# RWKV time mixing and a Fourier-mixed MLP on one core: the transposes of the last two batches made by DMA instead of TensorE

## The chip, the core and the metric

The kernel runs on one core of a Trainium2 chip. A core has five engines with a queue of instructions each: PE (TensorE, matrix products out of SBUF into PSUM), ACT (ScalarE), DVE (VectorE), POOL (GpSimd) and SP (SyncE, which here only issues DMAs). An engine takes its instructions strictly in order; between engines there are only semaphores. Transfers run on 16 DMA engines that all queues share. PSUM has 8 banks of 128 x 512 fp32, and only PE, ACT and DVE reach it in this kernel. The metric is device time in microseconds (us) of one execution; lower is better.

## The reference, cut to what matters

```python
# attention, (batch, heads, seq, head_dim) = (4, 8, 768, 48), one state matrix per head
for t in range(S):
    cur = einsum('bhd,bhe->bhde', u * kt, vt)
    y[:, :, t] = einsum('bhd,bhde->bhe', rt, state + cur)
    state = wt[..., None] * state + einsum('bhd,bhe->bhde', kt, vt)
# y is laid out as x (4, 768, 384), then
X = fft(fft(x, axis=1), axis=2)
u = x + real(X)
un = (u - mean(u)) / sqrt(var(u) + 1e-6)       # over the 384 features
out = u + relu(un @ w_ch1) @ w_ch2             # w_ch1 384 x 1536, w_ch2 1536 x 384
```

## The kernel before

**Attention.** Each batch has six chunks of 128 time steps, 24 chunks in all; chunk number n is 6 times the batch plus the chunk in the batch. A chunk's r, k, v and w arrive as four loads of 192 KB (L546), each in rows of 48 floats (192 bytes). The logarithm of w (L516, tile `lb`) is summed over time by two triangular matmuls (L707, L711) and exponentiated (L713, L726); r and k are multiplied by the results into bf16 tiles `rh` (L745, DVE) and `kh` (L502, mostly POOL), 128 time steps x 512 columns (8 heads padded to 64). TensorE contracts over partitions, so the product of k with r needs both with the head dimension on partitions: four transposes each of 128 x 128 against the identity (L756 for r, L762 for k) go to a PSUM bank, and one copy each (L525 on ACT or L526 on DVE) takes the bank to the SBUF tiles `rtb` and `ktb`. Eight matmuls (L773) then give the 128 x 128 products, DVE masks them into `ah` (L778), and the state (L796, L799, L807) and the output (L820, L823, L829) follow. L820 also reads `rtb`.

**Mix and MLP.** When a batch's six chunks are done, the Fourier transforms are matmuls against tables (L884 to L910). Each of six blocks of 128 rows is added to x (L912), its mean and variance are taken (L916, L918), the centred rows go to a bf16 tile `un` of 128 x 384 (L516 on ACT or L507 on DVE), three transposes on PE (L929) and one copy (L525 or L526) put them into `unt`. Three blocks make a half batch: 36 matmuls of the first layer (L951), the negative ReLU (L958 ACT, L956 DVE) and 36 of the second (L969), then the sum with u (L973) and the store (L977).

**Order.** Every instruction is recorded as an operation with its tiles. The order on each engine's queue is not found at run time: it is written out in the table `ORDER`, one list of operation numbers for each engine. At build time `schedule` walks those lists with assumed durations, only to assign PSUM banks, and `emit` puts a semaphore wait in front of an operation for what it depends on. So the engines run fixed lists, and a late operation holds everything behind it on its engine. SP's list holds all loads and stores; the weights of the two MLP layers are two DMAs on POOL's list (L685).

**Buffers.** There are 7 buffers for each loaded tensor and 3 each of `rh`, `kh`, `rtb` and `ktb`.

**The opening.** PE starts with 18 matmuls on scratch data (L990), and 20 pairs of matmuls whose result nobody reads (L1017, 384 columns each) are spread over its list in about the first 45 us.

Of the kernel before, what the change touches and what calls it, by code (L numbers as in the profile page):

```python
# [21 lines left out]

W_AFTER = {"W1": (0, 3, "w"), "W2": (1, 0, "r")}

W0, WP, NW = 8.0, 1.6, 20
# [4 lines left out]
        "72 6 99 125 127 1474 124 101 151 98 1475 153 64 68 137 111 110 136 114 203 1476 140 117 1477 177 179 "  # L30
        "143 150 119 205 163 176 66 189 162 145 1478 169 166 1479 188 1480 261 1481 1482 192 1483 202 171 215 "
        "195 228 229 262 197 214 1484 454 218 239 425 240 427 1485 456 243 1486 223 263 221 424 483 1487 1488 "
        "264 253 453 246 254 485 255 265 256 257 269 270 271 272 273 258 274 443 275 276 277 278 279 266 280 "
        "1489 437 292 301 436 302 303 283 293 294 284 465 312 285 313 466 330 314 1490 472 331 469 1491 332 1492 "
        "1493 440 308 299 321 290 322 323 475 361 341 347 349 482 355 345 357 351 353 337 343 328 359 446 363 "
        "495 319 365 370 366 494 512 511 371 498 501 514 367 386 382 372 523 504 380 384 545 524 546 548 530 390 "
        "527 557 388 375 558 533 578 564 376 579 561 775 377 777 398 589 394 590 392 396 566 593 402 400 404 774 "
        "596 804 787 603 604 405 611 619 806 786 803 406 790 620 605 606 621 622 623 612 607 608 624 625 626 627 "
        "613 614 628 629 630 615 616 651 793 815 633 642 652 653 634 635 643 644 662 409 816 833 663 832 835 410 "
        "411 822 819 414 664 658 415 640 649 796 416 825 695 693 709 713 697 845 844 851 699 701 691 848 711 896 "  # L40
        "862 864 898 705 669 703 671 672 861 673 895 707 854 715 874 929 716 873 680 717 681 877 725 907 880 908 "
        "720 940 682 911 883 721 928 1154 914 726 1156 1125 1127 678 916 722 939 1124 687 727 943 742 730 740 "
        "750 732 736 752 1183 738 734 953 1137 954 1143 946 1136 1185 744 746 1153 748 764 765 1140 1166 969 "
        "1165 1172 955 766 956 961 970 1169 957 971 972 973 1182 958 974 962 975 976 963 977 964 965 978 979 980 "
        "1201 1146 966 1212 992 1214 1195 1001 983 984 985 993 1002 1211 994 1003 1194 1012 759 1175 1246 754 "
        "1013 1014 1224 760 761 1198 1021 1022 1008 755 1279 999 1248 1230 990 1023 756 1245 1223 1204 1063 1053 "
        "1047 1041 1227 1043 1045 1030 1055 1031 1032 1257 1057 1233 1278 1051 1049 1258 1061 1070 1264 1028 "
        "1261 1059 1075 1289 1071 1290 1266 1065 1019 1293 1076 1066 1311 1037 1303 1067 1312 1077 1296 1082 "
        "1072 1090 1304 1319 1086 1096 1313 1094 1102 1305 1314 1320 1084 1321 1306 1322 1307 1315 1323 1316 "
        "1324 1308 1325 1092 1100 1342 1326 1327 1351 1328 1329 1333 1330 1088 1080 1098 1362 1334 1335 1371 "  # L50
        "1352 1104 1380 1343 1344 1353 1114 1363 1115 1364 1109 1381 1382 1372 1340 1110 1105 1373 1106 1358 "
        "1349 1111 1116 1401 1407 1403 1413 1411 1387 1395 1393 1369 1405 1397 1378 1391 1399 1432 1436 1444 "
        "1452 1440 1450 1430 1409 1415 1448 1420 1442 1434 1425 1446 1416 1421 1426 1422 1438 1427 1417 1459 "
        "1460 1461 1454 1464 1455 1456 1465 1466 1469 1470 1471"),
    "act": (
        "0 73 20 21 22 23 24 25 26 97 123 149 128 126 102 154 100 60 65 59 138 201 107 133 175 69 180 152 178 "
        "165 206 159 164 191 185 423 67 227 204 452 217 231 230 216 236 481 241 242 211 433 428 455 486 250 426 "
        "259 457 267 260 462 268 282 438 445 467 468 439 298 307 289 309 300 362 342 348 310 350 346 358 327 354 "
        "356 344 352 484 339 497 474 510 496 491 513 515 520 311 503 387 544 525 381 547 549 385 554 532 559 577 "
        "560 580 340 773 581 389 391 591 592 778 395 539 397 393 399 586 802 776 401 789 403 841 788 783 602 572 "  # L60
        "805 807 609 631 617 831 817 812 632 795 818 836 834 657 639 860 648 659 660 650 641 894 904 696 824 710 "
        "870 698 847 846 700 714 692 712 927 702 899 865 661 704 670 863 708 1123 897 931 876 853 909 910 942 "
        "882 1152 677 936 930 1181 679 686 941 1157 1126 1128 1210 889 689 731 1133 922 743 733 741 1162 737 739 "
        "735 1139 1191 1186 1138 1145 690 1155 747 749 751 952 1168 1167 1174 1220 959 1184 981 967 960 1244 "
        "1197 1215 1196 1213 1277 1203 1286 1226 998 1007 989 1009 1000 991 1010 1247 1281 1018 1249 1011 1048 "
        "1064 1042 1044 1046 1056 1259 1254 1232 1280 1052 1027 1050 1060 1239 1291 1062 1020 1036 1272 1038 "
        "1029 1083 1087 1091 1302 1309 1103 1093 1097 1331 1101 1317 1081 1039 1339 1357 1040 1360 1350 1341 "
        "1386 1370 1408 1379 1406 1404 1445 1414 1392 1361 1389 1398 1443 1437 1451 1390"),
    "dve": (
        "32 52 7 30 41 62 33 27 31 8 39 5 28 38 29 44 10 15 36 9 42 43 11 12 13 14 35 61 17 16 48 34 18 19 54 45 "  # L70
        "56 63 37 103 53 129 57 104 55 58 105 134 135 109 108 131 155 112 113 139 116 115 142 118 141 157 144 "
        "120 160 183 186 146 213 167 190 170 168 194 193 212 172 196 198 237 209 219 220 234 245 224 222 244 226 "
        "199 247 463 434 249 458 459 444 281 460 429 304 295 305 286 287 296 288 297 306 315 333 471 470 291 324 "
        "316 442 334 325 326 317 476 335 336 431 441 318 338 360 432 364 473 492 320 447 329 488 489 500 521 502 "
        "499 368 518 383 505 526 555 531 529 528 373 552 534 587 536 565 562 588 535 563 378 584 595 594 567 538 "
        "569 597 784 599 598 570 600 571 601 813 792 794 791 654 636 645 637 655 638 656 646 407 412 647 821 665 "
        "820 842 666 781 823 667 810 668 797 694 839 826 852 867 849 850 868 706 840 869 674 902 855 871 417 875 "
        "675 905 676 879 878 718 881 683 913 884 684 912 937 685 915 886 917 688 723 1131 919 945 934 887 1134 "
        "1160 728 944 753 1144 947 745 949 948 1163 1141 1142 1173 1171 1170 767 1147 1202 1192 986 995 1004 987 "
        "996 1005 997 1221 1006 988 1176 1015 762 1200 1199 1016 1189 1024 757 1017 1231 1255 1225 1218 1288 "  # L80
        "1205 1229 1228 1025 1054 1284 1026 1234 1252 1058 1260 1287 1265 1263 1033 1262 1237 1292 1034 1267 "
        "1035 1268 1294 1295 1285 1068 1270 1297 1298 1073 1271 1299 1078 1300 1085 1095 1099 1336 1089 1332 "
        "1354 1337 1345 1338 1355 1346 1356 1365 1366 1347 1383 1348 1384 1359 1374 1385 1375 1376 1367 1117 "
        "1368 1112 1402 1107 1412 1377 1388 1396 1394 1400 1431 1410 1453 1433 1441 1447 1449 1435 1439 1423 "
        "1428 1418 1462 1457 1467 1472"),
    "pool": (
        "4 1 2 3 51 46 50 130 40 47 161 156 49 181 132 182 106 187 158 122 184 121 207 208 148 147 232 174 238 "
        "233 210 173 200 235 225 251 435 248 464 252 430 493 461 487 490 516 517 522 519 550 556 551 553 582 583 "
        "537 585 785 568 610 808 814 809 837 618 779 838 780 843 782 811 866 932 900 901 872 903 1129 906 938 "
        "1130 1158 1159 933 885 918 1135 935 1164 888 1132 921 920 951 950 1193 1187 1161 982 968 1222 1188 1216 "  # L90
        "1250 1282 1217 1190 1219 1283 1251 1256 1236 1235 1253 1238 1269 1301 1310 1318"),
    "sp": (
        "71 77 75 78 74 79 70 81 82 87 83 80 89 86 76 85 84 90 88 92 419 91 448 93 94 477 96 420 95 422 449 478 "
        "450 421 451 479 506 480 507 508 509 540 542 541 543 573 769 575 574 770 576 771 828 798 772 830 827 801 "
        "800 374 799 829 369 856 893 923 924 859 891 890 858 379 857 925 892 1120 1121 1119 1149 1273 1180 408 "
# [286 lines left out]
def bass_rwkv6_finch__then__fnet_fourier_mix_kernel(  # L382
# [93 lines left out]
    def ps(t):  # L476
        return BANK[t.bank]
# [575 lines left out]
```

## Time and profile before

| what | value |
|---|---|
| median of 3 runs | 194.43 us (193.92 to 194.43) |
| the profiled execution | 194.31 us, of which the span of its profile is 192.5 us |
| PE | busy 181.3 us, 94% of the span, 1802 matmuls |
| DVE | 165.1 us, 86% |
| ACT | 131.7 us, 68% |
| POOL | 104.8 us, 54% |
| HBM | 23.59 MB read, 4.72 MB written |

Busy means that an instruction of the engine runs. PE's matmuls are pipelined: one of 128 columns is listed with 219 ns, but the next can start some 55 ns after it, so for PE the distance between starts is what a matmul costs. The span runs from the first to the last instruction of the profile; 1.8 us of the execution lie outside it.

### The profile page before, as it was taken

The numbers are of one execution on the slowest core, as the hardware profiler recorded it, in microseconds if no ns is written. First come the engines' busy times: TensorE is split into PE (matmuls) and PEld (weight loads), VectorE is DVE, ScalarE is ACT, GpSimd is POOL, SyncE is SP. The second block draws the span as 40 slices with busy tenths as digits, with TensorE's granted clock in tenths as the row PEclk, the third lists the DMA queues.
The fourth block names the chain that finished last, engine by engine and source line by source line (L and its number), as shares of the span: only waits on it lengthen the run. The fifth ranks groups of instructions, "written<-read, shape, count | busy, mean of one in ns | idle before, by whom it ended". The sixth has DMA issues, their size and how long they took to land.

```text
span 192.5 us, 4725 instructions
## 1 busy us (share of the span) xinstructions
PE 181.3 (94%) x1802; PEld 119.6 (62%) x1802; DVE 165.1 (86%) x374; ACT 131.7 (68%) x307; POOL 104.8 (54%) x123
## 2 busy tenths in 40 slices
PE   5886998899999988999999999999999999999994
PEld 2353766576666655667667676866666766665663
DVE  7888899999998999999999988999989939955353
ACT  4895877397887968998977898997944273243200
POOL 4069889673009856499799597976952230000000
PEclk9997899999999999999999999999999999999999
DMA  5999998999979999899949985102000300120033
GB/s 115 211 214 199 191 222 156 202 202 206 200 143 210 220 183 243 176 236 191 225 102 215 245 182 134 44 0 69 18 0 3 123 0 5 41 82 3 0 130 115
DMA packets 105416, 26.26 MB, mean 136 GB/s; under 512 B 100273, under 2 KB 105010, under 8 KB 105394
## 3 DMA queue, kind: packets, MB, share of 16 engines
q1 hardware_dynamic: 103442, 23.60, 57.4%
q0 software_dynamic: 1952, 2.36, 7.3%
q8 instruction: 14, 0.23, 0.5%
q14 instruction: 8, 0.07, 0.1%
HBM read 23.59 MB, written 4.72 MB: 147 GB/s over the span
## 4 chain that ended last, share of the span: by engine, by line
PE 78%; DVE 10%; SPq 6%; DMA 2%; issue 2%; ACT 1%; DVEq 0%
PE bank L969 24%; PE bank L951 24%; SPq L546 5%; PE bank L910 5%; PE bank L887 3%; PE bank L773 3%; DMA in_v<-in_v_dram 2%; PE bank L762 2%; DVE ah L778 2%; PE bank L823 2%; PE bank L929 2%; PE bank L756 2%; PE bank L707 2%; PE bank L799 2%; PE bank L820 2%; PE bank L711 2%
## 5 line engine op out<-in xcount | busy, mean ns | idle before, releaser
L969 PE MATMUL bank<-w,ht 128*128 128x384 bf16 (+2 forms) x300 | 55.1, 319 | 0.0
L951 PE MATMUL bank<-unt,w 128*128 128x384 bf16 x288 | 54.1, 326 | 0.0
L958 ACT ACTIVATE ht<-bank 128x384 bf16<-128x384 f32 x69 | 31.6, 496 | 11.2 <-PE bank L951 10.9
L969 PEld LDWEIGHTS bank<-w,ht 128*128 128x128 bf16 x300 | 27.5, 98 | 15.0 <-DVE ht L956 0.2
L951 PEld LDWEIGHTS bank<-unt,w 128*128 128x128 bf16 x288 | 26.4, 98 | 15.1
L778 DVE TENSOR_TENSOR ah<-bank,msk 128x512 bf16<-128x512 f32 x48 | 31.5, 680 | 1.6 <-PE bank L773 1.3
L502 POOL TENSOR_TENSOR vtd<-in_v,dc 128x384 f32<-128x384 f32 x20 | 17.2, 858 | 14.8 <-DVE dc L734 14.5
L502 POOL TENSOR_TENSOR rk<-rk,ub 128x384 f32<-128x384 f32 x20 | 20.5, 1032 | 7.8 <-DVE rk L502 7.4
L956 DVE TENSOR_SCALAR ht<-bank 128x384 bf16<-128x384 f32 x27 | 14.2, 549 | 12.2 <-PE bank L951 12.2
L502 POOL TENSOR_TENSOR kh<-in_k,e 128x384 bf16<-128x384 f32 x19 | 20.0, 1053 | 5.5 <-ACT e L726 5.4
L502 POOL TENSOR_TENSOR rk<-in_r,in_k 128x384 f32<-128x384 f32 x19 | 19.5, 1030 | 2.8 <-DVE dc L734 2.7
L973 DVE SCALAR_TENSOR_TENSOR osb<-bank,rstd,uf 128x384 f32<-128x384 f32 (+2 forms) x25 | 14.7, 593 | 4.1 <-PE bank L969 4.1
L525 ACT ACTIVATE rtb<-bank 128x512 bf16<-128x512 bf16 x20 | 12.0, 599 | 4.7 <-PE bank L756 4.5
L713 ACT ACTIVATE bank<-bank 128x384 f32<-128x384 f32 x24 | 11.8, 493 | 4.6 <-PE bank L707 4.4
L829 DVE TENSOR_TENSOR x<-bank,vtd 128x384 f32<-128x384 f32 x24 | 13.1, 547 | 1.2 <-PE bank L823 0.9
L745 DVE TENSOR_TENSOR rh<-bank,in_r 128x384 bf16<-128x384 f32 x24 | 13.1, 546 | 1.0 <-ACT bank L713 1.0
L516 ACT ACTIVATE vb<-in_v 128x384 bf16<-128x384 f32 x24 | 12.5, 525 | 2.1 <-DMA in_v<-in_v_dram 2.1
L912 DVE TENSOR_TENSOR uf<-bank,x 128x384 f32<-128x384 f32 x24 | 12.8, 547 | 0.6 <-PE bank L910 0.4
L525 ACT ACTIVATE unt<-bank 128x384 bf16<-128x384 bf16 x17 | 7.9, 491 | 7.8 <-PE bank L929 7.4
L734 DVE TENSOR_REDUCE dc<-rk 128x8 f32<-128x384 f32 x24 | 13.0, 540 | 0.2 <-POOL rk L502 0.2
L516 ACT ACTIVATE un<-uf,agg 128x384 bf16<-128x384 f32 x18 | 10.5, 608 | 3.8 <-DVE agg L918 3.8
L916 DVE BATCH_NORM_STATS2 bst<-uf 128x6 f32<-128x384 f32 x24 | 12.6, 546 | 0.1
(134 smaller groups left out, 383.2 us busy)
## 6 DMA issues: line engine op xcount, KB each, us to landing
in_w<-in_w_dram SPq DMA_DIRECT2D x24, 192.0 KB, 3.9
in_r<-in_r_dram SPq DMA_DIRECT2D x24, 192.0 KB, 3.8
in_k<-in_k_dram SPq DMA_DIRECT2D x24, 192.0 KB, 3.7
in_v<-in_v_dram SPq DMA_DIRECT2D x24, 192.0 KB, 3.8
out_dram<-osb SPq DMA_DIRECT2D x23, 192.0 KB, 2.0
w<-in_moe_w_ch_dram POOLq DMA_DIRECT2D x2, 1152.0 KB, 11.7
out_dram<-osb SPq DMA_DIRECT2D x1, 128.0 KB, 1.7
out_dram<-osb SPq DMA_DIRECT2D x1, 64.0 KB, 1.6
```

Source lines behind the costliest of these rows:

```text
L502: return lambda e: e.tensor_tensor(out=o, in0=a, in1=b, op=f)
L516: return lambda e: e.activation(o, a, f, **kw)
L525: {"act": lambda e: e.activation(o(), i(), ACTF.Copy), "dve": lambda e: e.tensor_copy(out=o(), in_=i())}, **kw)
L734: op("dve", v_1(DM), lambda e: e.tensor_reduce(out=dc[:, :], in_=rku[:, :, :], axis=mybir.AxisListType.X, op=ALU.add), r=[("RK", i2)], w=[ ...
L745: op("dve", v_1(DM), lambda e: e.tensor_tensor(out=rh[:, :, 0:D], in0=ps(tce)[:, 0:DM].rearrange("t (h d) -> t h d", d=D), in1=rt[:, :, :] ...
L778: masked[n] = op("dve", v_1(512), lambda e, x=x: e.tensor_tensor(out=ah[:, x:H:2, :], in0=ps(ta[x])[:, :].rearrange("p (h t) -> p h t", t= ...
L829: op("dve", v_1(DM), lambda e: e.tensor_tensor(out=xb[:, c, 0:DM], in0=ps(ty)[:, 0:DM], in1=vtd[:, :, :].rearrange("t h d -> t (h d)"), op ...
L951: ins = e.matmul(ps(t)[:, 0:384], W1[:, m, 128 * j:128 * j + 128], unt[:, m, :], start=(m == 0), stop=(m == NM - 1))
L956: {"dve": lambda e, j=j, t=t, ht=ht: e.tensor_scalar(out=ht[:, j, :], in0=ps(t)[:, 0:384], scalar1=-1.0, scalar2=0.0, op0=ALU.mult, op1=AL ...
L958: "act": lambda e, j=j, t=t, ht=ht: e.activation(ht[:, j, :], ps(t)[:, 0:384], ACTF.Relu, scale=-1.0)},
L969: ins = e.matmul(ps(t)[:, 0:hi - lo], ht[:, j, 128 * x:128 * x + 128], W2[:, j, lo:hi], start=(j == 0), stop=(j == NJ - 1))
L973: op("dve", v_1(hi - lo) + 64, lambda e, kb=kb, t=t, o=o, lo=lo, hi=hi: e.scalar_tensor_tensor(out=o[:, lo:hi], in0=ps(t)[:, 0:hi - lo], s ...
```

## The change

In chunks 12 to 23 (batches 2 and 3; `DMA_T = 12`) the eight PE transposes of `rh` and `kh`, their two PSUM banks and their two copies are gone. In their place SP issues two DMAs that transpose from SBUF to SBUF: `rh` to `rtb`, `kh` to `ktb`, each 128 x 512 in blocks of 128 columns. For batches 2 and 3 (`DMA_U = 2`) the three transposes of each `un` and the copy are replaced by one such DMA of 128 x 384. The new DMAs stand in SP's list, between loads and stores. `rh`, `kh`, `rtb` and `ktb` get a fourth buffer.

The matmuls that nobody reads become 14 single ones instead of 20 pairs, placed in other positions. The copy of the broadcast u (`UB`) must now come after the load of the second activation table. All five lists of `ORDER` are new, so operations that are otherwise untouched stand in other places, the opening included.

```diff
+DMA_T, DMA_U, T_ISSUE, T_XFER = 12, 2, 900, 600
-W0, WP, NW = 8.0, 1.6, 20
+NW = 14
 ORDER = {
...
+    NT = 4 if DMA_T < B * NC else 3
-    RH = [sb("rh%d" % i, [H, 64], BF16) for i in range(NB)]
+    RH = [sb("rh%d" % i, [H, 64], BF16) for i in range(NT)]
...
-        o = evict(lambda: UB[:, :, :]..., r=[t], w=["UB"])
+        o = evict(lambda: UB[:, :, :]..., r=[t, "LOGEXP"], w=["UB"])
...
+        if n >= DMA_T:
+            for x, o, i, y in ((rT, "RTB", rflat, "RH"), (kT, "KTB", kflat, "KH")):
+                op("sp", T_ISSUE, lambda e, x=x, i=i: e.dma_start_transpose(out=x[:, :, :], in_=i), r=[(y, i4)], w=[(o, i4)],
+                   sem="%s%d" % (o, i4), xfer=T_XFER)
+        else:
+            trr, trk = g.tile("a"), g.tile("a")
...
+            if b >= DMA_U:
+                op("sp", T_ISSUE, lambda e, un=un, unt=unt, kb=kb: e.dma_start_transpose(
+                    out=unt[:, :, 128 * (kb % 3):128 * (kb % 3) + 128], in_=un[:, :]),
+                   r=[("UN", n % 3)], w=[("UNT", (2 * b + hf) % 2, kb % 3)], sem="UNT%d" % (n % 6), xfer=T_XFER)
+            else:
+                tu = g.tile("f")
...
     for i in range(NW):
         def warm(e):
-            for x in range(2):
-                ins = e.matmul(ps(tw)[:, 0:384], MSK[:, :], IDW[:, :])
-            return ins
-        o = op("pe", mm(384, 2), warm, r=["MSK", "IDB"], w=[tw])
-        o.ready0 = int(1e3 * (W0 + WP * i))
+            return e.matmul(ps(tw)[:, 0:384], MSK[:, :], IDW[:, :])
+        o = op("pe", mm(384), warm, r=["MSK", "IDB"], w=[tw])
```

`T_ISSUE` and `T_XFER` are durations that `schedule` assumes for a transposing DMA; they set no instruction's time.

## The prediction

> **What bounds the kernel now.** I read the engines' shares and the slices first, then the windows, the chain of waits, PE's list in time, and the DMA queue.
>
> ```profile
> PE 181.3 (94%) x1802; PEld 119.6 (62%) x1802; DVE 165.1 (86%) x374; ACT 131.7 (68%) x307; POOL 104.8 (54%) x123
> DMA  5999998999979999899949985102000300120033
> PE 78%; DVE 10%; SPq 6%; DMA 2%; issue 2%; ACT 1%; DVEq 0%
> ```
>
> ```profile
> 0.00:60.00 60.00, 52.65 (x543) 33.53 (x544) 54.33 (x142) 44.18 (x97) 34.00 (x51) 0.97 1.01 189
> 60.00:120.00 60.00, 58.72 (x659) 39.69 (x659) 57.61 (x116) 52.23 (x127) 47.74 (x50) 1.00 0.94 198
> 120.00:192.50 72.50, 69.94 (x606) 46.34 (x606) 53.11 (x118) 35.27 (x85) 23.01 (x24) 1.00 0.12 42
> ```
>
> The windows' columns are PE, PE's weight loads, DVE, ACT and POOL busy, PE's granted clock, the DMA share and GB/s. From 60 us on PE has no room left, so a matmul removed there is time saved. In the same 60 to 120 us the DMA engines are full too (0.94); only after 120 us are they free (0.12). The change moves work from the full PE to a resource that is full for half of the affected time. In the first 60 us PE idles 7.4 us and is held by loads.
>
> **PE's transposes.** Starts in PE's list, in the full stage:
>
> ```profile
> 118.13 0.40 PE L762 MATMUL bank<-idw,kh 128*128 128x128 bf16 x4
> 118.37 0.25 PE L887 MATMUL bank<-cs,xf 128*128 128x193 bf16 x1
> 118.45 0.39 PE L756 MATMUL bank<-idw,rh 128*128 128x128 bf16 x4
> 118.67 0.33 PE L799 MATMUL bank<-vb,kh 128*128 128x96 bf16 x4
> ...
> 164.21 0.50 PE L929 MATMUL bank<-idw,un 128*128 128x128 bf16 x6
> 164.54 1.46 PE L969 MATMUL bank<-w,ht 128*128 128x384 bf16 x8
> ```
>
> Four transposes hold PE for 118.67 - 118.45 = 0.22 us, six of L929 for 0.33, so three for 0.165. Removed: 12 chunks x 2 x 0.22 = 5.3 us and 12 x 0.165 = 2.0 us, together 7.3 us, all behind 70 us, where PE is full. Bounds: a saving of 7.3, and none if PE then waits as long for the DMAs. I take -7.3 and cost the waits below.
>
> **Copies.** 24 copies of `rtb` and `ktb` at about 0.60 us (ACT) and 12 of `unt` at 0.49 leave ACT and DVE, some 20 us. I cost this at nothing: PE's matmuls cover it. If the cover went, DVE (57.61 of 60) would be next, and the copies off it are some slack there.
>
> **The DMA's own time.** No row shows a transposing DMA. The nearest is the load stage, by the DMA view of 60 to 118 us:
>
> ```profile
> DMA packets 53990, 11.84 MB, mean 204 GB/s; under 512 B 52830, under 2 KB 53982, under 8 KB 53982
> q1 hardware_dynamic: 53982, 11.73, 96.0%
> ```
>
> 58 us x 0.96 x 16 engines / 53982 = 16.5 ns a packet. A load (1024 rows of 192 bytes) is 64 packets an engine, 1.06 us. If a transpose moves one packet for each 128 bf16 columns of a row (256 bytes), 128 x 512 is 32 packets an engine, 0.53 us, and 128 x 384 is 0.40. The other end: if it is cut into 32-byte pieces, it has eight times the packets, 4.2 us. I take 0.55, because a 256-byte row is the packet nearest to the 192-byte rows that were measured, and keep both ends.
>
> What fits: without transposes the loads end at 118.8 (last issue 114.99, landing 3.8 later); the last L773 of attention starts at 144.6 and must come to about 138 if the gain is to be had. So 30 transposes (24, and 6 of batch 2's rows) share about 19 us of DMA time: 0.63 us each. Below that the DMA costs nothing, since the free stretch after 120 us takes it up; above it every 0.1 us costs 3 us. At 0.55 it fits by 2.5 us.
>
> **SP's queue and the added waits.** SP issues 36 more DMAs. An issue takes 0.33 us when the queue is empty (stores after 150 us) and 0.7 to 1.0 when it is full; bounds 0.33 to 1.5, taken 0.9; SP is idle after 120 us. But each transposing DMA waits on SP's list for its `rh` or `kh`, and the loads and stores behind it wait with it: the first transpose is SP's 62nd DMA, and 36 loads of batches 2 and 3 stand behind it, between the others. L773, with all of PE's list behind it, waits for the landing. Before, one such path is
>
> ```profile
> 117.51 0.54 DVE L745 TENSOR_TENSOR rh<-bank,in_r 128x384 bf16<-128x384 f32 x1
> 119.06 0.59 ACT L525 ACTIVATE rtb<-bank 128x512 bf16<-128x512 bf16 x1
> 119.92 0.40 PE L773 MATMUL bank<-rtb,ktb 48*128 48x128 bf16 x8
> out_dram<-osb SPq DMA_DIRECT2D x9, 192.0 KB, 3.2
> ```
>
> 1.9 us from `rh` to L773. The fourth line is the store's landing in the same full queue, 3.2 us. So a chunk's path grows by 1.3 us. Bounds: 0 (L745 stands far enough ahead) and 12 x 1.3 = 15.6 us (nowhere). PE's list holds MLP matmuls between, of 0.16 us each in hundreds, and `rh` has a fourth buffer to run ahead, so I stay near the low end: +1.5.
>
> **The opening.** On POOL's new list the first weights' DMA stands behind an `rk` product that waits for `in_r` buffer 6, and that load is now SP's 36th issue. Rows of before:
>
> ```profile
> 33.58 0.87 SPq L546 DMA_DIRECT2D in_r<-in_r_dram  x1
> 34.01 0.97 POOL L685 DMA_DIRECT2D w<-in_moe_w_ch_dram  x1
> 47.30 0.97 PE L951 MATMUL bank<-unt,w 128*128 128x384 bf16 x5
> ```
>
> The 36th issue starts at 33.58 and lands some 3.8 later, and the product takes 1.0: the weights would be asked for near 38 us instead of 34.01, and land 10.5 to 12.9 later, near 50 against the 47.30 at which L951 now starts. That is some 4 us, partly filled by attention matmuls. The ends are -1 (the new order of the loads helps chunk 0, whose `v` was waited for until 16.79) and +5. I take +3.0. The broadcast of u goes from SP's first issue to its ninth and stands ahead of the first L707, which was at 10.4; it lands near 10.4 too, which lies in the same delay. The 26 dropped filler matmuls (0.16 us each, 4.2 us) stood in idle time: nothing, but for the clock:
>
> ```profile
> 14.00:16.00 2.00, 1.01 (x15) 1.00 1.14 222
> 16.00:18.00 2.00, 0.95 (x14) 0.80 0.99 189
> 18.00:20.00 2.00, 2.00 (x21) 0.50 0.98 196
> 20.00:25.00 5.00, 5.00 (x68) 0.94 1.00 195
> ```
>
> These windows are of PE alone: busy, clock, DMA share, GB/s. After a half-idle stretch the granted clock is 0.80 and then 0.50, and it comes back by 25 us. Fewer fillers and a PE that waits for u may bring a second such stretch; 2 us at half clock lose 1 us of matmuls, but the opening is held by loads, so I take nothing for it, with 0 and +1 as ends. The Trainium skill, "TensorE: Matmul & The Clock Gate", Part 1, says that an idle window of about 3.4 us halves the clock, which speaks against dropping fillers; by that rule the sum below would be 192.5 us. The trace agrees in kind, with the 0.50 above.
>
> **Sum**, against the profiled 194.31 us (0.12 below the median): -7.3 (PE) +3.0 (opening) +1.5 (late landings) + 0 (DMA, copies, fillers) = -2.8, so 191.5 us.
>
> **Rivals.**
> (1) The DMA engines become the bound, slower. It decides when one transpose costs the 16 engines more than 0.63 us, and the whole is slower from about 0.63 + 2.8/30 = 0.72 us on. For it: 0.94 in the load stage, and a load's 16 parts that do not finish together, so that a transpose which needs all engines at once would hold those that are early. Against: 16.5 ns a packet. At 0.9 us each the cost is 30 x 0.27 = 8 us: 199.6 us; at 1.3 us, 211.6. The Trainium skill, "VectorE: DVE Perf Modes", "The three transpose paths", gives 1309 ns for one 128 x 128 block by DMA and 390 ns on TensorE and so advises TensorE; it stands on this rival's side.
> (2) The transposes are hidden but late: SP's waits hold loads back and L773 comes late in most chunks. For it: 3.2 us of landing against a 1.9 us path, and no slack in PE's list. Against: after 120 us a store lands in under 2 us. Half of the 15.6 us bound is +7.8 instead of +1.5: 197.8; at +4.5 it is 194.5, no change. I place it at 195.
> (3) The pieces are 32 bytes: 24 x 4.2 + 12 x 3.2 = 139 us more DMA work, with 19 us of room; over 300 us.
>
> **How the numbers follow.** 0.3% (0.6 us) is about what a measurement can tell here. My forecast, 189 to 193.8: 0.49. Rival 1, 196 to 212: 0.32. Rival 2, 193 to 198: 0.16. Rival 3: 0.03. Faster: nearly all of the forecast and a little of rival 2, 0.50; the same: 0.07; slower: 0.43. Range: the low end 188.8 (opening at +0.3 instead of +3.0), which leaves out 0.05; the high end 204 takes in rival 2 and the lower half of rival 1, up to about 1.05 us each, and leaves out 0.14. The likeliest case's own range is 189 to 193.8.
>
> **What the profile after would show.** Right: PE busy near 170 us, no rows for L929 in batches 2 and 3, PE still full from 60 us to the end, the transposing DMAs landing in 3 us or less, loads ending near 135 us, first L951 near 50 us. Rival 1: DMA share at 9 in all slices to 140 us and beyond, and idle PE ended by DMA `rtb` or `ktb`. Rival 2: the same waits, but gaps in the DMA row. Wrong altogether: if the issue itself holds SP for several us, which no row of before can show.

## The result and the profile after

The changed kernel is slower: 201.76 us median against 194.18 us of the kernel before on the same chip, a ratio of 1.039 (95% interval 1.036 to 1.042), where 191.5 us was forecast. Its profiled execution took 201.77 us, with a span of 200.0 us. Some executions, of the kernel before too, take over 1.5% longer than the fastest of the same kernel; the times below are medians of the others.

From the page of the changed kernel, the engines' shares, the slices of the granted clock and of the DMA engines, and the chain of waits:

```profile
PE 179.1 (90%) x1644; PEld 112.4 (56%) x1644; DVE 157.9 (79%) x353; ACT 120.0 (60%) x285; POOL 109.6 (55%) x132
PEclk9955999999999999999999889999699999999999
DMA  6999999999999975989998996987754011415033
...
PE 52%; DMA 16%; DVE 11%; ACT 6%; SPq 6%; POOL 5%; issue 3%; DVEq 0%; POOLq 0%; ACTq 0%
```

DVE and ACT did get rid of 7 and 12 us. PE's share of the chain fell from 78% to 52%, and transfers hold 16% of it, against 2% before. The windows of the changed kernel behind 60 us (PE, weight loads, DVE, ACT and POOL busy, granted clock, DMA share, GB/s):

```profile
60.00:120.00 60.00, 54.82 (x553) 34.99 (x552) 51.76 (x105) 41.42 (x102) 41.41 (x43) 0.97 0.91 183
120.00:200.00 80.00, 73.57 (x589) 46.19 (x586) 53.54 (x116) 35.59 (x89) 26.46 (x28) 0.98 0.44 101
```

Behind 60 us PE was idle for 3.8 us before (132.5 - 58.7 - 69.9); now it is idle for 11.6 us (140 - 54.8 - 73.6). The largest waits, in the list of waits of PE behind 60 us, and the transposing DMAs in the DMA view (median us from issue to landing at the end of the line):

```profile
PE bank L779 <- DMA rtb<-rh: 3.8, 3, 1.9
PE bank L962 <- DMA unt<-un: 2.2, 1, 2.2
```

```profile
rtb<-rh SPq DMA_TRANSPOSE x12, 2.5
...
unt<-un SPq DMA_TRANSPOSE x12, 2.4
```

Six of the 11.6 us are waits for transposing DMAs. Behind the two longest of them the granted clock falls as well (windows of PE alone: busy, clock, DMA share, GB/s):

```profile
113.00:117.00 4.00, 4.00 (x16) 0.58 1.03 242
140.00:144.00 4.00, 4.00 (x16) 0.57 0.75 163
```

The first stretch stands right behind a wait of 1.9 us for `rtb`, which ends at 112.4 us, and the second behind the 2.2 us for `unt`, which end at 139.4 us. A mean of 0.58 over 4 us is half clock for 3.4 us, so 1.7 us of matmul work are lost in each. In the kernel before, the clock is 1.00 from 25 us on.

The landings are as short as hoped. What is late is the issue. SP's queue in the timeline of the changed kernel (start, duration, instruction):

```profile
139.15 1.21 SPq L756 DMA_TRANSPOSE rtb<-rh  x1
140.40 0.58 SPq L548 DMA_DIRECT2D in_k<-in_k_dram  x1
141.02 1.56 SPq L756 DMA_TRANSPOSE ktb<-kh  x1
142.62 0.58 SPq L988 DMA_DIRECT2D out_dram<-osb  x1
143.25 1.22 SPq L756 DMA_TRANSPOSE ktb<-kh  x1
144.51 0.58 SPq L548 DMA_DIRECT2D in_r<-in_r_dram  x1
```

Each row begins 0.04 or 0.05 us after the end of the one ahead: SP waits for nothing here, it is busy issuing. A transposing DMA holds it for 1.2 to 1.3 us (1.56 in one row here, right behind a load), and a plain DMA behind one for 0.58. From 75 to 153 us this goes on almost without a gap, while in the kernel before SP's rows in 118 to 153 us are six stores. They are merged into one row, which holds the idle time between them too; each takes 0.33 to 1.01 us of issue:

```profile
122.20 29.95 SPq L977 DMA_DIRECT2D out_dram<-osb  x6
```

What the full queue does to chunk 22 is seen in three rows of the changed kernel, and in one of the kernel before, which stands last:

```profile
141.33 0.52 DVE L747 TENSOR_TENSOR rh<-bank,in_r 128x384 bf16<-128x384 f32 x1
149.03 1.27 SPq L756 DMA_TRANSPOSE rtb<-rh  x1
151.66 0.40 PE L779 MATMUL bank<-rtb,ktb 48*128 48x128 bf16 x8 [0.95 <-DMA rtb<-rh]
...
140.72 0.40 PE L773 MATMUL bank<-rtb,ktb 48*128 48x128 bf16 x8
```

`rh` is ready at 141.85, its transposition is issued 7.2 us later, and the eight matmuls of the chunk's products (L773 before, L779 now) start at 151.66 instead of 140.7. Loads stand in the same queue and come late too: POOL, which had no such waits behind 60 us before, waits 4.6 us there for `in_k` and 4.6 us for `in_r`.

The lag grows in two steps. The first half batch of the MLP's first layer (L951 before, L962 now) ends 3.6 us later than before, the next two 2.3 and 2.6, the fourth to the sixth 6.0, 6.7 and 8.5, and the last 9.2. So the opening costs about 3 us, as forecast, and another 6 us are lost between 97 and 157 us, just where 7 us should have been gained.

### The profile page after: what moved, and what is told of

The parts are those of the page before. It is cut to its first block, busy times and chain, and to the rows that moved or that the text cites. A ratio compares the mean times of both kernels' runs of the same rounds, so it can differ in the third digit from the quotient of the medians.

```text
span 200.0 us, 4398 instructions
## 1 busy us (share of the span) xinstructions
PE 179.1 (90%) x1644; PEld 112.4 (56%) x1644; DVE 157.9 (79%) x353; ACT 120.0 (60%) x285; POOL 109.6 (55%) x132
## 2 busy tenths in 40 slices
DMA packets 123462, 30.56 MB, mean 153 GB/s; under 512 B 118321, under 2 KB 123058, under 8 KB 123442
## 4 chain that ended last, share of the span: by engine, by line
PE 52%; DMA 16%; DVE 11%; ACT 6%; SPq 6%; POOL 5%; issue 3%; DVEq 0%; POOLq 0%; ACTq 0%
PE bank L962 21%; PE bank L980 16%; DMA w<-in_moe_w_ch_dram 6%; SPq L548 4%; DMA rtb<-rh 4%; DVE ah L784 3%; PE bank L893 3%; PE bank L779 3%; DMA in_r<-in_r_dram 2%; DMA in_v<-in_v_dram 2%; DMA unt<-un 2%; SPq L756 2%; PE bank L916 1%; POOL rk L504 1%; POOL vtd L504 1%
## 5 line engine op out<-in xcount | busy, mean ns | idle before, releaser
L962 PE MATMUL bank<-unt,w 128*128 128x384 bf16 x288 | 57.1, 340 | 2.5 <-DMA unt<-un 2.2
L969 ACT ACTIVATE ht<-bank 128x384 bf16<-128x384 f32 x80 | 36.9, 493 | 35.8 <-PE bank L962 35.6
L962 PEld LDWEIGHTS bank<-unt,w 128*128 128x128 bf16 x288 | 27.8, 101 | 21.8 <-issue 6.3
L504 POOL TENSOR_TENSOR kh<-in_k,e 128x384 bf16<-128x384 f32 x21 | 21.5, 1027 | 8.8 <-DMA in_k<-in_k_dram 4.6
L504 POOL TENSOR_TENSOR rk<-rk,ub 128x384 f32<-128x384 f32 x18 | 18.5, 1032 | 9.1 <-DVE rk L504 9.0
L779 PE MATMUL bank<-rtb,ktb 48*128 48x128 bf16 x192 | 9.8, 221 | 8.1 <-DMA rtb<-rh 3.8
L728 ACT ACTIVATE e<-bank 128x392 f32<-128x392 f32 (+1 forms) x24 | 11.8, 494 | 7.8 <-PE bank L722 5.2
L518 ACT ACTIVATE lb<-in_w 128x384 bf16<-128x384 f32 x24 | 12.5, 523 | 5.7 <-DMA in_w<-in_w_dram 5.6
L967 DVE TENSOR_SCALAR ht<-bank 128x384 bf16<-128x384 f32 x16 | 8.7, 548 | 8.0 <-PE bank L962 8.0
L504 POOL TENSOR_TENSOR xf<-sd 128x382 bf16<-128x382 f32 (+1 forms) x10 | 10.1, 1026 | 8.8 <-DVE sd L504 8.7
L779 PEld LDWEIGHTS bank<-rtb,ktb 48*128 48x128 bf16 x192 | 5.9, 95 | 14.5 <-issue 9.5
```

Source lines behind the costliest of these rows:

```text
L504: return lambda e: e.tensor_tensor(out=o, in0=a, in1=b, op=f)
L518: return lambda e: e.activation(o, a, f, **kw)
L779: ins = e.matmul(ps(ta[x])[:, 128 * q:128 * q + 128], kT[64 * x:64 * x + D, q, :], rT[64 * x:64 * x + D, q, :])
L962: ins = e.matmul(ps(t)[:, 0:384], W1[:, m, 128 * j:128 * j + 128], unt[:, m, :], start=(m == 0), stop=(m == NM - 1))
L969: "act": lambda e, j=j, t=t, ht=ht: e.activation(ht[:, j, :], ps(t)[:, 0:384], ACTF.Relu, scale=-1.0)},
```

## The experiments

**The theories.** S: SP is the bound from 75 to 153 us, since a transposing DMA's issue holds it for 1.26 us. D: the 16 DMA engines are full, as in the forecast's first rival. O: the new opening and the new order cost it all.

**Plain copies in place of the transposes.** The transposition is left out, so the output is not the reference's. Everything else, the lists included, is the changed kernel.

```diff
-    RTB = [sb("rtb%d" % i, [HP, 128], BF16) for i in range(NT)]
+    RTB = [sb("rtb%d" % i, [HP, 136], BF16)[:, :, 0:128] for i in range(NT)]
...
-    e.dma_start_transpose(out=x[:, :, :], in_=i)
+    e.dma_start(out=x[:, :, :], in_=i.rearrange("p (h t) -> p h t", t=128))
...
-    e.dma_start_transpose(out=unt[:, :, 128 * (kb % 3):128 * (kb % 3) + 128], in_=un[:, :])
+    e.dma_start(out=unt[:, :, 128 * (kb % 3):128 * (kb % 3) + 128], in_=un[:, :].rearrange("p (m t) -> p m t", t=128))
```

> The changed kernel, its order untouched, with each of the 36 transposing DMAs replaced by a plain DMA of the same bytes from the same tile to the same tile, in rows of 256 bytes (so that the transposition itself is left out; rtb and ktb get a pitch of 272 bytes so that the rows stay apart). Theory S (SP's issue is the price): an issue falls from the 1.2 to 1.3 us that the changed kernel shows to some 0.45, 36 x 0.8 = 29 us less on SP's queue, SP has gaps again from 75 to 153 us, and the time is 190 to 193.5 us (201.8 - 8.3 of late transposes and loads, which is the forecast's sum again). Theory D (the 16 DMA engines are full): the same packets and bytes, so 200 to 202 us, with the same DMA shares. Theory O (the new opening and the new order of PE cost it all): nothing of that is touched, 200 to 202 us.

Measured: 190.76 us, ratio to the kernel before 0.984 (0.978 to 0.990). The number of packets is that of the changed kernel within 0.5% (122886 against 123462). Most of the copies take 0.6 to 0.7 us of issue (0.69 on the mean of the 36, against 1.34 for the transposing DMAs). The window of 60 to 120 us, in which PE is full again, and SP's queue in its timeline:

```profile
60.00:120.00 60.00, 59.08 (x616) 38.14 (x613) 58.16 (x116) 47.06 (x116) 44.39 (x46) 1.00 0.94 197
```

```profile
131.37 0.60 SPq L756 DMA_DIRECT2D rtb<-rh  x1
132.01 0.64 SPq L548 DMA_DIRECT2D in_k<-in_k_dram  x1
...
134.45 0.60 SPq L756 DMA_DIRECT2D ktb<-kh  x1
```

What follows: with the same bytes, packets and lists the time falls by 11.0 us, to 0.7 us below the forecast. O falls as the cause of the whole. D falls as far as it goes by packets and bytes; that transposing bytes could cost the engines more than copying them is left to the merged kernel below.

**The same copies in three pieces each.** This puts the price of the issue back; the transposition is left out here too.

```diff
-    e.dma_start(out=x[:, :, :], in_=i.rearrange(...))
+    [e.dma_start(out=x[q, :, :], in_=i[q, :].rearrange("p (h t) -> p h t", t=128))
+     for q in (slice(0, 48), slice(48, 96), slice(96, 128))]
```

> As the plain copies, but each copy is issued as three DMAs (48, 48 and 32 partitions), with the same bytes and the same packets: 108 issues in place of 36, on the same place of SP's list. The transposition is left out here too. Theory S: three issues of 0.43 to 0.5 us are 1.3 to 1.5 us of SP, as much as one transposing DMA, so the time goes back to 200 to 204 us. Theory D: the engines' work is that of the plain copies, so the time is theirs, within 0.7 us. Theory O: 200 to 202 us, as the changed kernel and the plain copies.

Measured: 226.95 us, ratio 1.171 (1.160 to 1.182). SP's queue, three pieces to a row:

```profile
100.41 2.01 SPq L757 DMA_DIRECT2D ktb<-kh  x3
102.47 1.91 SPq L757 DMA_DIRECT2D rtb<-rh  x3
```

The direction is S's, and D's 190.8 is far off. The size was missed: I had taken 0.43 to 0.5 us for a piece, from plain loads behind a store, and a piece takes 0.60, so a copy holds SP for 2.0 us instead of 1.4. That makes a row of three prices for one issue at the same places of the same list: 0.65 us gives 190.8, 1.26 us gives 201.8, 2.0 us gives 227.0. Meanwhile the share of the DMA engines in 75 to 120 us falls to 0.68 and 0.70: they stand still for want of issues.

**The opening alone.** No transposing DMA, but the opening, the fillers and the fourth buffers of the changed kernel; the lists behind 55 us are arranged anew for the PE transposes that come back.

```diff
-DMA_T, DMA_U, T_ISSUE, T_XFER = 12, 2, 900, 600
+DMA_T, DMA_U, T_ISSUE, T_XFER = 24, 4, 900, 600
...
-    NT = 4 if DMA_T < B * NC else 3
+    NT = 4
```

> The changed kernel without any transposing DMA: all r, k and normed rows go through TensorE again, as in the kernel before, while its opening, its fillers, its fourth buffer of rh, kh, rtb and ktb stay; PE's, ACT's and DVE's lists behind 55 us are arranged anew for the work that comes back. Theory S and the forecast's term for the opening (+3.0): 196.5 to 198.5 us, with the first L962 of the MLP some 3 us later than before and the lag constant from there. Theory O: the whole loss is there without a transposing DMA, 200 us or more. If the opening costs nothing at the end: 194 to 195 us.

Measured: 196.43 us against 193.92, ratio 1.012 (1.008 to 1.016), 2.5 us. The first half batch of the first layer ends 3.5 us later than before and the last 1.8. O as the cause of the whole falls again; as a term of the sum its size was right.

**Two edits of that opening.** On POOL's list the weights' DMA (253) ahead of where it stands; on SP's list the fetch of u (73) first.

```diff
 "pool"
-... 437 237 202 212 201 431 253 228 254 ...
+... 437 253 237 202 212 201 431 228 254 ...
```

> The opening alone (no transposing DMA), with one edit: on POOL's list the first weights' DMA is moved five places ahead, so that it is asked for near 34 us as in the kernel before, and no longer stands behind the rk product that waits for in_r buffer 6. The forecast's mechanism of the +3.0 (the weights asked for 5 us late, and the first L951 with them): the first MLP layer starts near 47.5 us again and the time is 194 to 195 us. Its rival (the weights were in time; what holds the opening is the loads and chunks 6 and 7, whose r comes late): asking for 1.1 MB five us earlier, among loads that keep the engines full, pushes in_r back further; 197 to 201 us.

```diff
 "sp"
-76 72 81 80 83 79 77 84 73 87 85 78 ...
+73 76 72 81 80 83 79 77 84 87 85 78 ...
```

> The opening alone (no transposing DMA), with one edit: the DMA that fetches u goes back from SP's ninth issue to its first. In the opening alone PE waits 4.3 us for it at the bonus matmul, near 10 us. If that wait is part of the +3.0: 195 to 196 us. If the opening is held by the loads that come behind (in_r of chunks 4 to 6), the 4.3 us come back as waits for them, and the time stays at 196.7 within 0.7 us; the clock of 0.66 in 10 to 15 us should then be 1.0 and make no difference either.

Measured: the weights earlier 205.37 us, ratio 1.063 (1.055 to 1.072), slower than both expectations; u first 196.34 us, ratio 1.016 (1.010 to 1.022). POOL in the timeline of the opening alone, and then with the weights earlier (its profiled execution took 209 us, so the order is to be read there, and not the last us):

```profile
38.26 0.99 POOL L441 TENSOR_TENSOR rk<-in_r,in_k 128x384 f32<-128x384 f32 x1 [1.28 <-DMA in_r<-in_r_dram]
39.19 0.98 POOL L624 DMA_DIRECT2D w<-in_moe_w_ch_dram  x1
```

```profile
35.23 0.99 POOL L624 DMA_DIRECT2D w<-in_moe_w_ch_dram  x1
...
49.40 0.99 POOL L441 TENSOR_TENSOR rk<-in_r,in_k 128x384 f32<-128x384 f32 x1 [4.49 <-DMA in_r<-in_r_dram]
```

Asked for 4 us earlier, the weights take the room of loads that are needed first: the next `rk` product waits 4.5 us for its r, ACT waits 9.9 us for an `in_v`, and chunk 6, which starts its products at 47.8 in the opening alone, starts them at 59.5. So the weights' late request is no slip that can be put right by itself: in this order of the loads it has to be late. The 4.3 us that PE waits for u in the opening alone are gone when u is fetched first; a wait of 2.3 us for the copy of the broadcast u has come in their place, and the time stays within its scatter, so no cost of that wait is seen. The clock of 10 to 15 us stayed at 0.66, where 1.0 was expected, so this run tells nothing of the clock. Which part of the new order of the loads costs the 2.5 us stays open.

**One DMA for r and k together.** The decisive one: real transpositions, the same bytes, 12 issues fewer.

```diff
+    RKH = [sb("rkh%d" % i, [2, H, 64], BF16) for i in range(NT)]
+    RH, KH = [x[:, 0] for x in RKH], [x[:, 1] for x in RKH]
...
-            for x, o, i, y in ((rT, "RTB", rflat, "RH"), (kT, "KTB", kflat, "KH")):
-                op("sp", T_ISSUE, lambda e, x=x, i=i: e.dma_start_transpose(out=x[:, :, :], in_=i), ...)
+            op("sp", T_ISSUE, lambda e: e.dma_start_transpose(out=RKTB[i4].rearrange("p x h t -> p (x h) t"),
+                                                              in_=RKH[i4].rearrange("t x h d -> t (x h d)")),
+               r=[("RH", i4), ("KH", i4)], w=[("RTB", i4), ("KTB", i4)], ...)
```

> The changed kernel with r and k of a chunk side by side in one tile, and one transposing DMA of 128x1024 for both in place of two of 128x512, at the place of the later of the two on SP's list; the normed rows' 12 transposing DMAs stay, and nothing else is moved. The same bytes go through the 16 DMA engines. Theory S, and an issue that costs about the same whatever its size (1.18 us for 128x384 and 1.21 to 1.28 for 128x512 in the changed kernel with an empty queue): the issue takes 1.3 to 1.6 us, SP is rid of 12 x 1.0 = 12 us or more, and the time is 192.5 to 197 us. Theory S, and an issue that costs by the 128x128 block: 2.4 us each, nothing saved on SP, 200 to 204 us, since r then also waits for k. Theory D (the 16 engines): the same work, 200 to 204 us.

Measured: 192.68 us against 193.58, ratio 0.995 (0.992 to 0.998). SP's queue in its timeline:

```profile
133.61 1.36 SPq L692 DMA_TRANSPOSE rktb<-rkh  x1
...
139.79 1.31 SPq L692 DMA_TRANSPOSE rktb<-rkh  x1
```

The issue costs about the same for 128x1024 as for 128x512: six of the 12 take 1.24 to 1.36 us, and of the other six (1.64 to 2.12 us) five stand right behind a load, where single ones are longer too (1.36 to 1.76 us). Here the median landing is 3.6 us, and 9.1 us of the loss are gone with 12 issues. PE's waits for transposing DMAs behind 60 us fall from 6.0 to 2.0 us. D falls now for transposing bytes too. The share of q1 on the page (the queue of SP's DMAs) times the span is the time that its packets took on the engines: 110.8 us in the opening alone, 137.0 in the changed kernel, 136.5 here. The engines do the same work in the slow and in the fast one.

Adding up the durations of the rows that SP starts in the 78 us from 75 to 153 shows where its list is full. With some 0.045 us between rows, the 73.6 us of the changed kernel's 77 issues leave about 1 us of the 78:

| kernel | SP issuing, of 78 us | time |
|---|---|---|
| before | 36.3 | 194.2 |
| plain copies | 57.1 | 190.8 |
| r and k merged | 60.5 | 192.7 |
| three pieces | 72.6, and 34.4 more behind | 227.0 |
| changed | 73.6 | 201.8 |

**A version that beats both.** The fillers of the kernel before and an opening near to its own (SP's first loads stand in another order, and the first half batch of the MLP ends 0.3 us earlier than before), and transposing DMAs only where SP and the DMA engines have room: batch 3's r and k, merged, and the normed rows of batches 2 and 3.

```diff
-DMA_T, DMA_U, T_ISSUE, T_XFER = 12, 2, 900, 600
+DMA_T, DMA_U, T_ISSUE, T_XFER = 18, 2, 1330, 620
...
-NW = 14
+W0, WP, NW = 8.0, 1.6, 20
```

> The kernel before, with its own opening and its own fillers, and transposing DMAs only where SP has room: r and k of chunks 18 to 23 (batch 3 alone), one DMA of 128x1024 for both, and the normed rows of batches 2 and 3, 12 DMAs of 128x384. The lists behind 40 us are arranged anew for it. Theory S: 18 issues of 1.2 to 1.35 us, 23 us, most of them behind 115 us, where SP of the kernel before issues for 2.8 of 33 us, so nothing waits for SP; PE is rid of 12 x 0.22 + 12 x 0.165 = 4.6 us; 189.5 to 191.5 us against 194. If a landing of 2.4 to 3.6 us on the path of the chunk and of the half batch costs as much as PE saves: 193.5 to 196. Theory D: the engines are free there (share 0.12 before), so as S.

> As the one of batch 3, but from chunk 15 on: 9 chunks merged, and the normed rows of batches 2 and 3. PE is rid of 18 x 0.22 + 2.0 = 6.0 us, but three of the merged DMAs and their 128 KB each now lie between 97 and 115 us, where loads fill the DMA engines and SP. Theory S with the measured price (1.3 us a merged issue; 4 us more of SP there): 188.5 to 191 us, about 1 us better than from chunk 18. Theory D (engine time of 0.74 us for each 128x512, 9 units of it more in the full stretch, some 4 us of loads pushed back): no better than from chunk 18, or up to 3 us worse.

> The one of batch 3, with r and k of each chunk transposed by two DMAs of 128x512, one right behind the other, in place of one of 128x1024; nothing else differs. 6 issues of 1.26 us more, 7.6 us, all behind 110 us, where SP has room. Theory S says that the price of an issue matters only where SP is full: within 1 us of the merged one. If each issue delays its chunk whatever SP's load (the second of the two lands 1.3 us later, six times, nothing else to do on PE): up to 6 us slower than the merged one.

Measured against 193.77 us: from chunk 18, merged, 190.25 us, ratio 0.982 (0.979 to 0.984); from chunk 15, merged, 190.58 us, 0.984 (0.982 to 0.987); from chunk 18, unmerged, 191.31 us, 0.986 (0.983 to 0.989). The windows of the first, and the wait of PE for a transposing DMA behind 60 us:

```profile
60.00:120.00 60.00, 58.55 (x653) 39.75 (x651) 58.51 (x118) 50.55 (x126) 48.03 (x50) 1.00 0.95 193
120.00:190.00 70.00, 65.42 (x524) 41.40 (x521) 44.32 (x97) 31.32 (x77) 25.19 (x27) 1.00 0.35 83
```

```profile
PE bank L718 <- DMA rktb<-rkh: 0.4, 1, 0.4
```

Behind 60 us PE is busy for 124.0 us, against 128.7 before: 4.7 us less, as 12 x 0.22 + 12 x 0.165 = 4.6 us says. Of these, 3.5 arrive in the time, and PE waits for a transposing DMA 0.4 us in all; its largest wait there is 1.4 us for DVE's `rkh`. The lists behind 40 us were arranged anew, and no run has the new lists without the DMAs, so the 3.5 us are the gain of both together. Unmerged, SP issues 6.6 us more in 120 to 153 us (22.9 against 16.3 of 33), and the time is 1.1 us longer in the medians, with intervals that touch: six issues cost 1.1 us where SP has room, and twelve cost 9.1 us in the changed kernel, where it has none. The extension to chunk 15 missed its expectation of another 1 us. It tells nothing of the DMA engines, though: its first half batch of the MLP is already 2.1 us late at 56 us, ahead of any transposing DMA, so its lists differ from the other's where the change isn't.

## Why the prediction was wrong

**The failed step is SP's queue.** It said: "An issue takes 0.33 us when the queue is empty ... and 0.7 to 1.0 when it is full; bounds 0.33 to 1.5, taken 0.9; SP is idle after 120 us", and the sum had no term for it. The price was 1.18 to 1.28 us where no load stood right ahead, and 1.34 on the mean of the 36, inside the bounds. What was left out was the addition that the same prediction made for the DMA engines: what fits. The rows of before had all of it. From 75 us to 144.6 us, when the last L773 started, are 69.6 us; SP issues for 33.5 us of these in 75 to 120 us and 2 us behind. The rest, 34.1 us, is for 30 transposing DMAs: 1.14 us each. At 0.9 they fit with 7 us to spare; at 1.26 they need 37.8 us, 3.7 us too much, and at the 1.36 us that the first 30 took on the mean 40.9, 6.8 too much. The deciding price lay inside the bounds, so this was a rival to be named, with a chance that is anything but small. The prediction's last sign of being wrong, an issue that holds SP for several us, had the right place and a size too large: 1.3 us, 36 times, was enough. The surplus is only the floor: chunk 23 starts its products 10.2 us later than before. Loads and transposes that wait for each other share the one list, and the half clock behind PE's waits adds 3.4 us; how the rest is divided was not measured. The plain copies, with issues of 0.65 us, show the term that was missing: 201.76 - 190.76 = 11.0 us.

The Trainium skill, "Perfetto Trace Analysis", section What "DMA-bound" means, lists the issuing engine's sequencer as a bound of its own, beside the DMA engines: its track is then solid with DMA slices, which show the making of descriptors and not the moving of data. The trace agrees: SP's rows from 139.15 on are solid, and a row of 256 KB is some 0.1 us longer than one of 128 KB where no load stands right ahead.

**PE's transposes, -7.3, and late landings, +1.5.** Right in their sum, once SP's issue is taken out: from the opening alone (196.43) to the plain copies (190.76) are -5.7 us, where these two terms add up to -5.8. The two were not measured apart, and the lists of the opening alone differ behind 55 us, so the agreement to 0.1 us is partly luck. In batch 3 alone PE's 4.6 us were measured as 4.7. That PE would be busy near 170 us was wrong: 179.1. Most of the 9 us between them are the clock, by an estimate from the granted clock of the windows: it is 0.5 for 10.2 us of the opening, against 3.4 us in the kernel before, and for twice 3.4 us behind PE's waits. These 13.6 us at half clock are 6.8 us of matmul work.

**The opening, +3.0.** The size was right (2.5 us), and in the changed kernel the chain of waits runs as the working had it, as these lines of the chain in 24 to 62 us show (start, duration, what):

```profile
38.83 11.31 DMA w<-in_moe_w_ch_dram
...
50.28 4.06 PE bank L962 x24
```

The weights are asked for at 38.83 (forecast: near 38) and L962 starts at 50.28 (near 50). But the forecast took the request behind the `rk` product for the cause, and asking earlier, alone, made it worse: the loads need the room. So the size came out with a cause that is not shown.

**The DMA engines' own time, 0.55 us and a bound of 0.63.** The packets are those assumed, not 32-byte pieces, so the third rival was rightly small. But the size was low: (137.0 - 110.8) / 36 = 0.73 us each. By the first rival's rule that made the engines the bound, and the merged kernel, with the same engine time, is 0.5% faster than before. The rule counted the engines' share of 0.94 as full, while the windows reach 1.01 to 1.04; 0.63 was no limit. Nor had the last products to start near 138 us for the gain to be had: in the plain copies they start at 145.0, and the time is 190.8. So the rival that held 0.32 of the chance came close to the time, and with another cause.

**The second rival** (late, with gaps in the DMA row, 193 to 198 us; the time lies above its range) had the right picture: waits for `rtb`, and loads held back on SP. It laid them to SP's waits for `rh` and `kh`. The plain copies wait for the same tiles at the same places of the list, and their time is 0.7 us below the forecast; it is the time that each issue takes.

**Copies off ACT and DVE, fillers, clock: 0.** DVE and ACT lost 7 and 12 us of work, and no gain from it is seen. No run took the fillers alone.

## What to carry to other kernels

A queue that only issues DMAs is a resource like an engine: add up its issues in the stretch where they must be done, with the price of the new kind as the unknown, and work out the price at which they no longer fit. Here a transposing DMA cost SP 1.2 to 1.4 us for three, four or eight blocks of 128 x 128, so two that go together should be one, and they belong where both the queue and the DMA engines have room. Swapping the operation for a cheaper one of the same bytes, in the same place, separates the queue from the engines in one run.

## What the runs showed of the hardware

- An issue of a transposing DMA from SBUF to SBUF, behind an idle queue, a store or one of its own kind, holds SP in most cases for 1.18 to 1.26 us at 128x384, 1.20 to 1.28 at 128x512 and 1.24 to 1.34 at 128x1024; right behind a load it is mostly 1.36 to 2.1 us.
- A plain DMA from SBUF to SBUF of the same rows takes 0.59 to 0.69 us of issue in 29 of 36 cases (up to 1.28 in the others), and some 0.60 when it is cut to a third; a store takes 0.33 on an idle queue and 0.58 right behind a transposing DMA.
- The transposing DMA lands 2.4 to 3.2 us after its issue (medians of the three tiles in the changed kernel), 3.6 us for 128x1024 in the merged one. By the differences of q1's packet time, an estimate, it costs the 16 engines 0.73 us on the mean of 128x512 and 128x384, and a plain copy of the same bytes 0.59 us ((132.1 - 110.8) / 36).
- Behind waits of PE of 1.9 and 2.2 us the granted clock fell to half for 3.4 us, twice, though PE had been busy for 1.5 and 1.2 of the 3.4 us ahead.
